# Re-placing the attention and token-mixing steps between the channel-mixing matmuls of a fused pooling-attention and MLP-mixer kernel

## The chip, the cores and the metric

The kernel runs on one core of one Trainium2 chip. Times are device microseconds (us) of one execution. Of several executions of a kernel the median is quoted. Executions of one program mostly agree within a few tenths of a per cent; a few are 1 to 2% longer, at a slightly lower granted clock of TensorE (0.987 to 0.993, where the others have 0.997 to 1.0), and these slow ones are left out of every comparison. The kernel before took 280.01 us (median of 3 runs, 279.32 to 280.36).

Engines: PE is TensorE (matrix products and transposes), DVE is VectorE, ACT is ScalarE, POOL is GpSimd, SP issues transfers. "L258" is line 258 of the kernel.

## The reference, cut to what matters

```python
# q, k, v: [8 batches, 8 heads, 576, 64]
k_p = k.reshape(B, H, 72, 8, D).mean(axis=3)          # keys and values pooled by 8
v_p = v.reshape(B, H, 72, 8, D).mean(axis=3)
attn = softmax(q @ k_p^T / 8)                          # 576 x 72
x = concat_heads(attn @ v_p)                           # [8, 576, 512]
h = relu(x^T @ w_tok1) @ w_tok2                        # token mixing, 576 -> 256 -> 576
u = x + h^T
out = u + relu(u @ w_ch1) @ w_ch2                      # channel mixing, 512 -> 1536 -> 512
```

The channel mixing of one batch is 96 matmuls of 512 columns, about 20.7 us of TensorE. All the rest of a batch takes far less of TensorE, but it takes DVE, ACT and GpSimd as well.

## The kernel before: the parts that the argument touches

The channel mixing of batch n is "unit n". It is cut into 48 steps of two matmuls each, 0.43 us a step. Between the steps the kernel places pieces of the other work for the batches that follow, so that TensorE always has something to do while the other engines prepare. Unit 8 is the rows that are left over from all batches.

```python
ps_one = ... tile_pool(bufs=3, space=PSUM)   # products of 512 columns
ps_two = ... tile_pool(bufs=2, space=PSUM)   # scores and AV, two banks each
ps_tr  = ... tile_pool(bufs=1, space=PSUM)   # transposes: one buffer for all of them
...
def unit_steps(n, st):                       # the stream: 48 steps of two matmuls
    for m in range(NM):                      # NM = 12
        ps = ps_one.tile([P, 512], FP32, name="p1")
        for kk in range(4):
            nc.tensor.matmul(out=ps, lhsT=w_ch1[...], rhs=uT[:, kk, :], ...)        # L445
            if kk == 1:
                yield
        nc.scalar.activation(out=GT[:, m, :], in_=ps, func=AF.Relu)                 # L449
        yield
    ...                                      # then 48 matmuls with w_ch2, L467, and the stores
def unit(n, at):                             # `at` is the plan: step -> pieces
    for i, _ in enumerate(unit_steps(n, ...)):
        for s in at.get(i, "").split():
            ...   # "<x": for batch n, "x": for batch n+1, ">x": for batch n+2; "lk3": load k of batch n+3
```

The pieces that a plan can name, as they are in both kernels:

```python
K0 K1 V0 V1   pool8: three adds on GpSimd for half the heads (L145, L146, then L149 or L151)
Q0..Q3        qD: 32x32 block transposes of the queries on DVE (L246)
kpT           four transposes of the pooled keys on TensorE (L194), a copy to SBUF on ACT (L196)
s0 s1 s2      score4 on 32-row tiles of the array (L258, tile_position=(l*32, 0)): 8 matmuls of 512
              columns in s0 and s1, 16 of 64 in s2; then two exponentials on ACT (L263)
av0..av4      8 matmuls exp x values (L297), then reciprocal and product on DVE (L309, L315)
at0 at1       first token mixing: 5 matmuls (L343), then a relu on ACT (L334) or DVE (L336)
u0..u4        second token mixing: 2 matmuls (L358), then the addition of x on DVE (L359)
t0..t4        four transposes of u on TensorE (L368), a copy on DVE (L369)
M0 M2 M4 M    the other way of transposing u: written to HBM, read back in blocks ("bounce"),
T0..T4        then block transposes on DVE (L390)
lk lq lv      loads of k, q and v, issued from GpSimd's queue
```

Every engine works through its pieces in the order of the plan. A plan therefore fixes who waits for whom.

The softmax here doesn't subtract the row's maximum and nothing guards it: scores larger than these inputs give would overflow.

## Time and profile before

| | before |
|---|---|
| median time | 280.01 us |
| profiled span | 278.3 us |
| TensorE busy, by the page | 97% |
| units 1 to 6, by the trace | 174.61 us |
| of this the floor (instructions times their quiet spacing) | 169.10 us |
| lost in units 1 to 6 | 5.51 us |

The prediction below shows how the floor was counted. Two things of the page help to read it. Here are, of the kernel before, the row of the chain that ended last by engine, and two rows of the costliest groups (count, then busy us and mean ns of one, then idle time before and what ended it):

```profile
PE 83%; DMA 8%; ACT 3%; DVE 2%; POOL 2%; issue 1%; POOLq 0%
...
L449 ACT ACTIVATE GT<-p 128x512 bf16<-128x512 f32 x108 | 64.0, 599 | 75.8 <-PE p L445 75.6
...
L359 DVE TENSOR_TENSOR u<-p,x 128x512 bf16<-128x512 f32 x32 | 22.1, 691 | 13.9 <-PE p L358 13.6
```

TensorE is only 83% of the chain: in the rest something else held the end back, part of it in the head and unit 0, part in small waits in the units. The two rows give the time that ACT (599 ns) and DVE (691 ns) need to empty a PSUM bank of 512 columns.

### The profile page before, as it was taken

The numbers are of one execution on the slowest core, as the hardware profiler recorded it, in microseconds if no ns is written. First come the engines' busy times: TensorE is split into PE (matmuls) and PEld (weight loads), VectorE is DVE, ScalarE is ACT, GpSimd is POOL, SyncE is SP. The second block draws the span as 40 slices with busy tenths as digits, with TensorE's granted clock in tenths as the row PEclk, the third lists the DMA queues.
The fourth block names the chain that finished last, engine by engine and source line by source line (L and its number), as shares of the span: only waits on it lengthen the run. The fifth ranks groups of instructions, "written<-read, shape, count | busy, mean of one in ns | idle before, by whom it ended". The sixth has DMA issues, their size and how long they took to land.

```text
span 278.3 us, 4495 instructions
## 1 busy us (share of the span) xinstructions
PE 268.9 (97%) x1790; PEld 130.9 (47%) x1824; DVE 141.8 (51%) x272; ACT 111.2 (40%) x187; POOL 130.8 (47%) x121
## 2 busy tenths in 40 slices
PE   8989999999999999999999999999999999999994
PEld 3755445444543545454445444544454444444443
DVE  5465967771575757275178545834584161011012
ACT  2543590039305533614741366046604602602600
POOL 8585222999996992898069999600000000000000
PEclk9999999999999999999999999999999999999999
DMA  7999999980299930793549562324132545015024
GB/s 162 185 203 206 205 203 187 225 179 10 24 180 180 231 50 0 138 218 89 115 74 241 144 129 49 77 66 126 38 78 57 136 71 115 0 39 113 2 44 108
DMA packets 36837, 32.68 MB, mean 117 GB/s; under 512 B 14288, under 2 KB 30288, under 8 KB 36816
## 3 DMA queue, kind: packets, MB, share of 16 engines
q0 software_dynamic: 18672, 17.64, 40.2%
q1 hardware_dynamic: 17984, 14.62, 20.9%
q8 instruction: 14, 0.23, 0.3%
q10 hardware_dynamic: 160, 0.13, 0.2%
q14 instruction: 7, 0.06, 0.1%
HBM read 38.21 MB, written 11.80 MB: 180 GB/s over the span
## 4 chain that ended last, share of the span: by engine, by line
PE 83%; DMA 8%; ACT 3%; DVE 2%; POOL 2%; issue 1%; POOLq 0%
PE p L467 32%; PE p L445 30%; PE p L358 6%; PE p L343 5%; DMA kr<-in_k_dram 5%; PE p L258 4%; PE p L297 3%; DMA f<-in_moe_w_tok_dram 3%; ACT ex L263 1%; PE pt L368 1%; PE p L479 1%; ACT GT L449 1%; DVE o L453 1%; POOL vr L86 1%; POOL kr L86 1%
## 5 line engine op out<-in xcount | busy, mean ns | idle before, releaser
L467 PE MATMUL p<-w_ch,GT 128*128 128x512 bf16 x404 | 99.2, 379 | 1.0 <-issue 0.3
L449 ACT ACTIVATE GT<-p 128x512 bf16<-128x512 f32 x108 | 64.0, 599 | 75.8 <-PE p L445 75.6
L445 PE MATMUL p<-uT,w_ch 128*128 128x512 bf16 x373 | 92.7, 379 | 1.1 <-issue 0.3
L445 PEld LDWEIGHTS <-w_ch 128*128 128x128 bf16 x432 | 40.3, 98 | 48.1 <-issue 4.9
L467 PEld LDWEIGHTS <-GT 128*128 128x128 bf16 x420 | 38.0, 98 | 41.9 <-issue 3.1
L453 DVE TENSOR_TENSOR o<-p,u 128x512 f32<-128x512 f32 x32 | 21.9, 684 | 31.4 <-PE p L467 31.2
L263 ACT ACTIVATE ex<-p 72x1024 bf16<-72x1024 f32 (+1 forms) x42 | 31.6, 807 | 10.8 <-PE p L258 10.8
L146 POOL TENSOR_TENSOR t<-t 72x512 f32<-72x512 f32 x24 | 30.3, 1262 | 1.9
L145 POOL TENSOR_TENSOR t<-kr 72x1024 f32<-72x1024 bf16 x12 | 25.5, 2123 | 8.5 <-DMA kr<-in_k_dram 7.8
L359 DVE TENSOR_TENSOR u<-p,x 128x512 bf16<-128x512 f32 x32 | 22.1, 691 | 13.9 <-PE p L358 13.6
L145 POOL TENSOR_TENSOR t<-vr 72x1024 f32<-72x1024 bf16 x12 | 25.4, 2120 | 0.9
L390 DVE STREAM_TRANSPOSE uT<-v 128x512 bf16<-128x512 bf16 x16 | 10.4, 686 | 23.7 <-DMA v<-mem 23.7
L334 ACT ACTIVATE AT<-p 128x512 bf16<-128x512 f32 x8 | 4.8, 597 | 42.0 <-PE p L343 39.2
L315 DVE TENSOR_TENSOR x<-p,den 128x512 bf16<-128x512 f32 x30 | 20.7, 691 | 1.0
L246 DVE STREAM_TRANSPOSE qD<-qb 128x576 bf16<-128x576 bf16 x28 | 20.5, 794 | 0.0
L297 PEld LDWEIGHTS <-ex 72*128 72x128 bf16 x320 | 15.3, 98 | 10.4 <-DVE x L315 0.8
L358 PE MATMUL p<-AT,w_tok 128*128 128x512 bf16 x63 | 18.8, 379 | 0.0
L297 PE MATMUL p<-vp,ex 72*128 72x65 bf16 x320 | 16.8, 194 | 1.0 <-DVE x L315 0.6
L309 DVE RECIPROCAL den<-p 128x8 f32<-128x8 f32 (+1 forms) x39 | 7.9, 203 | 17.5 <-PE p L297 16.6
L103 POOL DMA_DIRECT2D qb<-in_q_dram x7 | 5.1, 730 | 21.5 <-DVE qD L246 20.3
L343 PE MATMUL p<-x,w_tok 128*128 128x512 bf16 x54 | 14.1, 379 | 0.1
L336 DVE TENSOR_SCALAR AT<-p 128x512 bf16<-128x512 f32 x8 | 5.5, 692 | 13.4 <-PE p L343 12.6
(90 smaller groups left out, 206.4 us busy)
## 6 DMA issues: line engine op xcount, KB each, us to landing
out_dram<-o SPq DMA_DIRECT2D x70, 128.0 KB, 2.5
kr<-in_k_dram POOLq DMA_DIRECT2D x7, 576.0 KB, 11.8
qb<-in_q_dram POOLq DMA_DIRECT2D x7, 576.0 KB, 11.1
vr<-in_v_dram POOLq DMA_DIRECT2D x7, 576.0 KB, 15.2
w_ch<-in_moe_w_ch_dram POOLq DMA_DIRECT2D x6, 512.0 KB, 13.2
mem<-u SPq DMA_DIRECT2D x8, 256.0 KB, 2.1
v<-mem SPq DMA_DIRECT2D x8, 160.0 KB, 3.8
v<-mem SPq DMA_DIRECT2D x8, 128.0 KB, 3.0
```

Source lines behind the costliest of these rows:

```text
L145: eng.tensor_tensor(out=t4[:, 0:n], in0=t[:, hs, 0:4], in1=t[:, hs, 4:8], op=ALU.add)
L146: eng.tensor_tensor(out=t4[:, 0:n, 0:2], in0=t4[:, 0:n, 0:2], in1=t4[:, 0:n, 2:4], op=ALU.add)
L263: nc.scalar.activation(out=exv[:, a, :, gs.start:gs.stop, n0:n0 + n], in_=pss[a][0:SP, :, 0:len(gs) * n].rearrange("j l (g n) -> j l g n", ...
L297: nc.tensor.matmul(out=halves[h // 4][:, (h % 4) * (D + 1):(h % 4 + 1) * (D + 1)], lhsT=st["ex"][:, h * S + n0:h * S + n0 + P], rhs=st["vp ...
L315: nc.vector.tensor_tensor(out=dst.rearrange("p (a h d) -> p a h d", a=2, d=D), in0=view[:, :, :, 0:D], in1=den[rows, :, :, None].broadcast ...
L343: nc.tensor.matmul(out=ps, lhsT=w_tok1[:, c if c < 4 else 4 + par, m * P:(m + 1) * P], rhs=st["x"][:, c, :] if c < 4 else st["xt"], start= ...
L358: nc.tensor.matmul(out=ps, lhsT=w, rhs=a, start=(i == 0), stop=(i == len(mms) - 1))
L359: nc.vector.tensor_tensor(out=dst, in0=ps, in1=x, op=ALU.add)
L445: nc.tensor.matmul(out=ps, lhsT=w_ch1[:, kk, m * P:(m + 1) * P], rhs=uT[:, kk, :], start=(kk == 0), stop=(kk == 3))
L449: nc.scalar.activation(out=GT[:, m, :], in_=ps, func=AF.Relu)
L453: nc.vector.tensor_tensor(out=o_sb, in0=ps, in1=(u_tails if n == B else st["u"])[:, c, :], op=ALU.add)
L467: nc.tensor.matmul(out=pss[c], lhsT=GT[:, m, c * P:(c + 1) * P], rhs=w_ch2[:, m, :], start=(m == 0), stop=(m == NM - 1))
```

## The change

The intent is to place the pieces by a model of when each engine gets to them, so that TensorE meets nothing unfinished. Only the plans of units 1 to 8 are different; `HEAD` and `FIRST` (head and unit 0) are wrapped in other places of the text and have the same words. Both programs have the same 1,824 matmuls, loads and stores. `LATER` serves units 4 to 8; in 7 and 8 no later batch is left to place.

```diff
-    SECOND = {0: "Q0 Q1", 1: "kpT Q2 Q3 >K0 >K1 lk3 lq3 lv3 >V0 >V1", 4: "s0", 8: "s1", 13: "s2", 15: "av0", 17: "av1",
-              19: "av2", 21: "av3", 23: "av4", 25: "at0", 26: "at1", 28: "u0", 29: "u1", 30: "u2 t0", 32: "u3 t1", 34: "t2 >Q0",
-              36: "t3 >Q1", 38: ">Q2 >Q3", 39: ">kpT", 40: ">s0 lk4 lq4 lv4", 44: ">s1"}
-    THIRD = {0: ">K0 >K1 >V0 >V1 s2", 2: "av0", 4: "av1", 6: "av2", 8: "av3", 10: "av4", 12: "at0 >Q0", 13: "at1",
-             15: "u0", 16: "u1", 18: "u2 t0", 19: "u3", 20: "t1 u4", 22: "t2 >Q1", 24: "t3", 26: "t4", 27: ">Q2 >Q3",
-             28: ">kpT lq4 lk4 lv4", 29: ">s0", 33: ">s1", 37: ">s2", 39: ">av0", 41: ">av1", 43: ">av2", 45: ">av3", 47: ">av4"}
-    FOURTH = {0: ">K0 >K1 >V0 >V1 at0", 1: "at1", 3: "u4 M4", 4: "u0", 6: "u1 M0", 7: "u2", 9: "u3 M2 M",
-              15: ">Q0", 17: ">Q1", 18: ">kpT", 22: ">s0", 26: "T0", 27: ">Q2 >Q3 lq4 lk4 lv4", 29: "T1", 31: "T2", 32: ">s1",
-              33: "T3", 35: "T4", 37: ">s2", 39: ">av0", 41: ">av1", 43: ">av2", 45: ">av3", 47: ">av4"}
-    LATER = {0: ">K0 >K1 >V0 >V1 at0", 1: "at1", 3: "u4 M4", 4: "u0", 6: "u1 M0", 7: "u2", 9: "u3 M2 M",
-             15: ">Q0", 17: ">Q1", 18: ">kpT", 22: ">s0 >Q2", 24: ">Q3", 27: ">s1", 28: "T0", 30: "T1", 31: "T2",
-             33: ">s2 T3", 35: "T4", 37: ">av0", 39: ">av1", 41: ">av2", 43: ">av3", 45: ">av4"}
+    SECOND = {0: ">K1 Q0 lq3 kpT Q1 Q2", 1: "lv3", 3: "s0 lk3 >V0", 4: ">K0", 6: "Q3 >V1", 8: "s1", 13: "s2",
+              16: "av1 av0", 19: "av2", 20: "av3", 22: "av4", 24: "at1 at0", 26: "u0", 28: ">Q0", 29: "u1", 30: "t0",
+              31: "u2", 32: "t1", 33: "u3 t2", 35: "t3", 36: ">Q1", 37: ">kpT", 38: "lq4", 39: ">s0 >Q2",
+              40: ">Q3 lv4", 44: ">s1", 45: "lk4"}
+    THIRD = {0: ">V0 >K1", 1: "s2", 2: ">K0 >V1", 3: "av0 av1", 6: "av3", 7: "av2", 9: "av4", 10: "at0",
+             12: "at1 >Q0", 15: "u0", 16: "u1", 17: "u2 t0", 18: "u4", 19: "t1", 21: "u3", 22: "t2", 24: ">Q1",
+             25: "t3", 27: "lq4 >kpT", 28: "lv4", 29: "lk4 >Q3 >s0 >Q2", 32: "t4", 33: ">s1", 38: ">s2", 40: ">av0",
+             41: ">av2", 43: ">av1", 45: ">av3", 47: ">av4"}
+    FOURTH = {0: "M4 u4 >K1", 1: "at0 at1 >K0", 3: "u0 >V0", 5: "u1 M0", 6: ">V1", 7: "u2", 8: "u3 M2", 9: "M",
+              15: ">kpT >Q1", 17: ">Q0", 22: "lq4", 25: ">Q2", 26: ">s0", 27: "T0", 28: ">Q3 lk4 lv4", 29: "T1",
+              32: ">s1 T2", 34: "T3", 37: ">s2", 38: "T4", 39: ">av0", 41: ">av1", 42: ">av2", 45: ">av3", 46: ">av4"}
+    LATER = {0: ">K1 at0", 1: "at1", 2: ">V1", 3: "u1 >V0", 5: "u0 u2 u4 >K0", 7: "M0 M4", 9: "u3", 10: "M2", 11: "M",
+             14: ">Q0", 17: ">Q1", 20: ">kpT", 22: ">s0", 25: ">Q2", 26: ">Q3", 27: "T0 >s1", 28: "T3", 31: "T2 T1",
+             35: ">s2", 37: ">av1 >av0", 38: "T4", 41: ">av2", 45: ">av3", 46: ">av4"}
```

In words: the key transposes and the first score group of unit 1 come one step earlier; AV of unit 1 starts one step later after the third score group; u and t pieces are spread; key transposes and first scores of the next batch get more distance; the last score group and AV of units 4 and 5 are closer together; in units 3 to 6 the u pieces are shifted against the channel mixing; query loads go before value and key loads; pools come in another order in all of units 1 to 5.

## The prediction

> **What bounds the kernel now.** I read four views in this order: the page's busy shares and slices, the busy time by window cut at the borders of the nine units of channel mixing, the chain that ended last, and the waits with the timeline of each engine around the places where the chain left TensorE. First the page, engine shares and two rows of its 40 slices:
>
> ```profile
> PE 268.9 (97%) x1790; PEld 130.9 (47%) x1824; DVE 141.8 (51%) x272; ACT 111.2 (40%) x187; POOL 130.8 (47%) x121
> PE   8989999999999999999999999999999999999994
> PEclk9999999999999999999999999999999999999999
> ```
>
> TensorE (PE) is busy in every slice, the clock is full, and no other engine is over 51%. The ends of matmuls are modelled, though, so 97% does not say how much is left. For that I took the distance from one matmul's start to the next. Pieces of the chain (start us, length us, what):
>
> ```profile
> 59.31 0.29 PE pt L194 x4
> 59.60 1.30 PE p L445 x6
> 60.90 0.61 PE p L258 x8
> 61.51 1.91 ACT ex L263 x2
> ...
> 67.66 0.28 ACT ex L263
> ...
> 85.20 0.41 ACT kD L196
> ...
> 88.11 0.80 PE p L258 x8
> ...
> 122.87 0.68 DVE xt L315
> ...
> 136.58 0.56 PE p L258 x8
> ...
> 157.21 0.51 PE p L358 x2
> 157.72 0.43 PE p L445 x2
> ...
> 216.63 6.04 PE p L445 x28
> ```
>
> 28 matmuls of 512 columns took 6.04 us: 0.2157 us each when nothing is missing. The same reading gives 0.0325 us for an AV matmul (8 in 0.26), 0.056 for a 128-column transpose, 0.13 for the four key transposes (L194), 0.56 for a quiet score group of 512 columns and 0.26 for one of 64 (144.38, x16). The reader should see the exceptions: a score group of 0.80 instead of 0.56, a pair L358 of 0.51 instead of 0.43, and pieces of ACT and DVE, where TensorE stood waiting.
>
> Now the windows of units 1 to 6 (window, length, busy us and count by engine, clock, DMA share, GB/s):
>
> ```profile
> 58.26:90.14 31.88, 31.11 (x225) 14.24 (x228) 17.74 (x34) 15.38 (x25) 28.29 (x24) 1.00 0.61 105
> 90.14:122.09 31.95, 31.47 (x265) 16.05 (x270) 19.81 (x41) 13.72 (x23) 24.72 (x20) 1.00 0.63 120
> 122.09:150.20 28.11, 27.90 (x193) 12.83 (x193) 15.48 (x31) 12.41 (x20) 17.40 (x15) 1.00 0.59 127
> 150.20:179.33 29.13, 28.72 (x196) 13.23 (x197) 17.88 (x35) 12.41 (x20) 26.84 (x21) 1.00 0.56 119
> 179.33:207.24 27.91, 27.59 (x187) 12.84 (x190) 15.73 (x30) 12.41 (x20) 0.00 (x0) 1.00 0.31 76
> 207.24:232.87 25.63, 25.44 (x118) 11.55 (x119) 10.09 (x16) 7.66 (x13) 0.00 (x0) 1.00 0.40 88
> ```
>
> **The floor of each unit** is its instructions times those spacings. Unit 1: 96 channel matmuls 20.72, ten of the first token mixing 2.16, eight of the second 1.73, 16 transposes 0.89, two key transposes 0.26, four score groups of 512 columns 2.24, one of 64 0.26, forty AV 1.30: 29.56 us. In the same way units 2 to 6 come to 30.96, 27.41, 28.29, 27.41 and 25.47. Taken from the window lengths this leaves 2.32, 0.99, 0.70, 0.84, 0.50 and 0.16, together **5.5 us that units 1 to 6 lose**. Units 7 and 8 run at the floor; head and unit 0, 58.26 us, aren't changed.
>
> **What the Trainium skill says.** "TensorE: Matmul & The Clock Gate", section "Back-to-back issue gap", gives N / 2.4 + 2.5 ns for a warm matmul, 215.8 ns at N = 512; the trace agrees (215.7). The same section puts a sustained stream with weight loads at about 131 ns; this stream has a weight load per matmul and doesn't reach it. "Perfetto Trace Analysis", "Identifying the Most-Contended Engine", says that matmul busy share is no measure of the room left; the trace agrees, as a matmul is listed at 379 ns and the next starts after 216. Its "Optimization Strategy" says that a gap that repeats can mean too few PSUM buffers; the 0.51 above is one. "PSUM — Partial Sum Buffer", "Engine vs sequencer instructions", says that the queues of ACT, DVE and GpSimd are strictly first in, first out, and that matmuls start in program order. The trace agrees: a query load sat up to 9.9 us at the head of GpSimd's queue until DVE's transposes of the queries had freed its buffer. So order decides who waits, and the change is one of order alone.
>
> **The change.** The programs of both kernels hold the same instructions: 1,824 matmuls, the same loads and stores, no byte more. It can't lower the floor, only move the 5.5 us. Of them about 0.10 us go at the entry of each of 18 score groups (steps of the actual time against the floor, also where no engine was late): 1.8 us, in both kernels. At most 3.7 us can be won. By unit (a plan's step is two matmuls, 0.43 us; positions are floor time since the unit began, and I chose to compare such distances rather than to add up waits of other engines):
>
> - Unit 1, front. The transposes of the keys move from step 1 to step 0, to 0.43 us, but their PSUM buffer is freed by a DVE copy that ended at 59.25, about 1.0 into the unit. Their wait grows from 0.19 to some 0.62: a loss of 0.43. The first score group still waits for the second query transpose (near 60.8). In return the second score group no longer meets unfinished exponentials (0.25), nor does the third (0.19), and AV starts 1.56 after the third score group instead of 1.13, which saves most of the 0.38 of the wait at 67.66. Net about +0.1.
> - Unit 1, rear. A u/t pair is spread (0.08 + 0.17 + 0.19), and key transpose to score goes from 0.56 to 1.00, where transpose, copy and score need some 0.8 (0.22 lost at 85.20 today). The next group comes 2.71 after it instead of 2.28, so that two exponentials of 1.93 together fit between (0.25 at 88.11). DVE will be dense there; I leave 0.25. Net +0.5.
> - Unit 2: key transpose to score 0.56 to 0.99 (0.22), score to score 2.28 to 2.51 (0.25). Net +0.45.
> - Units 3 and 4: the tail of x came late to the first token mixing, 0.21 and 0.36 (the chain's 122.87 and its like at 151.12). Unit 3 now starts that mixing 0.43 later, and unit 3's own last AV, for unit 4, is issued 0.43 earlier. At the end of unit 4 the last AV is 0.43 later, at 27.59 of 28.29: with one reciprocal (0.21) and two products of 0.69 behind it x is there about 0.9 into unit 5, before it is read at 1.30. Net +0.55.
> - Units 3 to 6, u steps: today a matmul reuses a PSUM bank 1.08 after the bank's last matmul and DVE's add of 691 ns stands between, which misses by 0.08, twice in a unit. In the new order the reuse at 1.08 is of a bank that ACT empties in 597 ns, which fits. Four units at 0.16: +0.6.
>
> Sum: 0.1 + 0.5 + 0.45 + 0.55 + 0.6 = 2.2 us. I take off 0.2 for new small waits: **2.0 us, 278.0 us**.
>
> **Rivals.**
> 1. GpSimd becomes the bound. In units 4 and 5 the new order pools K1, V1, V0, K0, where it was K0, K1, V0, V1, so the keys are complete after four pools instead of two. One pool is 2.12 + 1.26 + 0.72 plus gaps, 4.34 us. For it: unit 4's pools queue behind the query load that waits for DVE (began 141.56, now about 0.7 earlier, as one transpose leaves the way). With two more issues of about 0.8 they start near 143.3 and end near 160.7. Against it: the key transposes stand at 13.81 in a unit that begins at 150.2, near 163.5. Slack is about 3 us; if the load slips behind the bounce by 5 us, 2 us are lost and the time is 280.
> 2. DVE gets stuck. The block transposes of the bounced u come first in line one step earlier (27), and wait for the same transfer, issued after the same last add (DVE stood 23.7 us in four such waits already). Query transposes placed behind them would hold up scores. In units 4 and 5 all four now stand ahead; in unit 3 one stays behind, but the score group that needs it hasn't moved (18.82). Cost if I misjudge: about 0.5 us in each of three units, 279.
> 3. The exponentials come late for AV. In unit 4 AV followed the small score group by 1.99, in the new order by 1.12. At the same 1.12 in unit 2 the trace shows AV at 117.34 without a wait, because ACT had no relu in its queue. Same here; else 0.2 a unit.
> 4. Transfers move the time. Query loads go ahead of value and key loads and start up to 4 us earlier; the keys they feed are needed a unit later, and the DMA share in these windows is 0.31 to 0.63. Hidden either way.
>
> **Range and chances.** All waits won that can be: 276.3. Nothing won, or rival 1 or 2 eating the gain: 280. A wait missed in every unit of three: 281. Runs of one kernel spread by 1 us here (279.32 to 280.36). I set 278.0, with 276.8 to 279.8 for 8 in 10. Faster by over 2% needs 5.6 us, more than all that is lost in the changed units above the score entries, 3.7: chance 0.01. Slower by over 2% needs a systematic stall of about 1 us in each changed unit; I found no chain that gives it: 0.02.
>
> **What would show it.** PE's busy share stays at 97% and counts stay the same. Units 1 to 6 should be about 31.3, 31.5, 27.75, 28.65, 27.75 and 25.5 us long. Key transposes at the head of unit 1 should wait longer than 0.19; ACT's exponentials, the copy of the keys and the tail of x should leave the chain from unit 2 on; pairs of L358 should take 0.43. The prediction is wrong if a key transpose waits for a pool in unit 4 or 5, if a score group waits for a query transpose after unit 1, or if AV waits for exponentials in units 4 and 5.

## The result, and the profile after

| | before | after |
|---|---|---|
| median, fast runs | 280.23 us (6 runs, 279.32 to 280.45) | 277.38 us (5 runs, 276.67 to 277.46) |
| slow runs left out | none | one, 283.1 us |
| ratio of fast runs, after / before | | 0.9896, 95% interval 0.9877 to 0.9915 |
| profiled span | 278.3 us | 275.7 us |
| lost in units 1 to 6 | 5.51 us | 2.80 us |

A ratio here is the mean time of one kernel's fast runs over the mean of the other's fast runs in the same rounds on the same chip; it is therefore not quite the ratio of the medians. The change takes 1.0% off. 277.4 lies in the predicted range of 276.8 to 279.8, 0.6 us below the 278.0.

Of the kernel after, two rows of the page: the busy shares (those of before are in the prediction) and the chain that ended last by engine:

```profile
PE 268.2 (97%) x1824; PEld 130.4 (47%) x1824; DVE 141.4 (51%) x272; ACT 111.3 (40%) x187; POOL 130.9 (47%) x121
...
PE 94%; DMA 2%; DVE 2%; issue 0%; POOL 0%; ACT 0%; POOLq 0%
```

The busy share of TensorE is the same 97% to the digit, and tells nothing of the gain. The chain tells more: ACT has left it, and TensorE has gone from 83% to 94%. But about half of this rise lies in the unchanged head and unit 0, where the chain of after runs through 5.6 us of loads instead of 22.6. From unit 1 on, ACT and DVE hold 12.2 us of the chain before and 1.4 us after. A chain shows what held the end back, not how much was lost; that is read from the units.

The trace of before lists 1,790 of its 1,824 matmuls, that of after all of them. A missing record makes a piece look as if it waited, so I read the waits of both from the starts of neighbouring instructions.

The windows of units 1 to 6 of the kernel after (window, length, busy us and count by engine in the order PE, weight loads, DVE, ACT, POOL, then clock, DMA share, GB/s):

```profile
58.36:89.29 30.93, 30.45 (x230) 14.05 (x229) 17.62 (x34) 15.30 (x25) 26.32 (x22) 1.00 0.62 103
89.29:120.71 31.42, 31.42 (x272) 15.86 (x270) 19.54 (x40) 13.82 (x23) 23.34 (x19) 1.00 0.63 114
120.71:148.46 27.75, 27.75 (x196) 12.86 (x193) 15.82 (x30) 12.56 (x20) 20.39 (x17) 1.00 0.71 148
148.46:177.06 28.60, 28.60 (x196) 13.24 (x195) 17.24 (x34) 12.41 (x20) 25.67 (x20) 1.00 0.52 112
177.06:204.79 27.73, 27.73 (x191) 12.82 (x190) 15.58 (x30) 12.41 (x20) 0.00 (x0) 1.00 0.33 79
204.79:230.26 25.47, 25.47 (x119) 11.53 (x118) 10.64 (x18) 7.66 (x13) 0.00 (x0) 1.00 0.40 88
```

Each line answers to one of the six in the prediction. The lengths sum to 171.90 us against 174.61, a gain of 2.71. Unit 1 begins 0.10 later than in before (58.36 against 58.26), and from the end of unit 6 to the end both take 45.4. So 2.71 less 0.10 is the 2.6 us between the spans: **the gain lies in the six changed units and nowhere else**.

| unit | length before | predicted | after | lost before | lost after |
|---|---|---|---|---|---|
| 1 | 31.88 | 31.3 | 30.93 | 2.32 | 1.37 |
| 2 | 31.95 | 31.5 | 31.42 | 0.99 | 0.46 |
| 3 | 28.11 | 27.75 | 27.75 | 0.70 | 0.33 |
| 4 | 29.13 | 28.65 | 28.60 | 0.84 | 0.32 |
| 5 | 27.91 | 27.75 | 27.73 | 0.50 | 0.32 |
| 6 | 25.63 | 25.5 | 25.47 | 0.16 | 0.00 |

The front of unit 1 in the chain of the kernel after (start us, length us, what):

```profile
59.41 0.29 PE pt L194 x4
59.71 1.30 PE p L445 x6
61.00 0.56 PE p L258 x8
61.56 2.27 PE p L445 x10
...
68.34 0.52 PE p L297 x16
```

The score group at 61.00 takes its quiet 0.56 (0.61 in before) and is followed by matmuls, where before had ACT's exponentials on the chain at 61.51. At 67.66 before had an exponential ahead of AV; here AV runs at its quiet pace. Left in this part is only the wait ahead of the key transposes at 59.41.

### The profile page after: what moved, and what is told of

It is laid out like the page before. It is cut to its first block, busy times and chain, and to the rows that moved or that the text cites. A ratio compares the mean times of both kernels' runs of the same rounds, so it can differ in the third digit from the quotient of the medians.

```text
span 275.7 us, 4525 instructions
## 1 busy us (share of the span) xinstructions
PE 268.2 (97%) x1824; PEld 130.4 (47%) x1824; DVE 141.4 (51%) x272; ACT 111.3 (40%) x187; POOL 130.9 (47%) x121
## 4 chain that ended last, share of the span: by engine, by line
PE 94%; DMA 2%; DVE 2%; issue 0%; POOL 0%; ACT 0%; POOLq 0%
PE p L445 34%; PE p L467 33%; PE p L358 6%; PE p L343 5%; PE p L297 4%; PE p L258 4%; DMA kr<-in_k_dram 2%; PE pt L368 1%; PE p L479 1%; PE p L225 1%; PE pt L515 1%; PE p L277 1%; PE p L326 1%; PE p L408 1%; PE p L203 1%
## 5 line engine op out<-in xcount | busy, mean ns | idle before, releaser
L467 PE MATMUL p<-w_ch,GT 128*128 128x512 bf16 x420 | 101.3, 379 | 0.0
L145 POOL TENSOR_TENSOR t<-kr 72x1024 f32<-72x1024 bf16 x12 | 25.5, 2121 | 6.7 <-DMA kr<-in_k_dram 5.9
L145 POOL TENSOR_TENSOR t<-vr 72x1024 f32<-72x1024 bf16 x12 | 25.5, 2121 | 0.8
L297 PEld LDWEIGHTS <-ex 72*128 72x128 bf16 x320 | 14.7, 98 | 9.1 <-DVE x L315 1.1
L358 PE MATMUL p<-AT,w_tok 128*128 128x512 bf16 x64 | 18.5, 379 | 0.0
L334 ACT ACTIVATE AT<-p 128x512 bf16<-128x512 f32 x8 | 4.8, 597 | 34.1 <-PE p L343 31.3
L297 PE MATMUL p<-vp,ex 72*128 72x65 bf16 x320 | 16.1, 194 | 0.5 <-DVE x L315 0.3
L258 PE MATMUL p<-qD,kD 32*72 32x512 bf16 (+1 forms) x224 | 11.4, 294 | 0.0
```

The source lines that it names most:

```text
L145: eng.tensor_tensor(out=t4[:, 0:n], in0=t[:, hs, 0:4], in1=t[:, hs, 4:8], op=ALU.add)
L258: nc.tensor.matmul(out=pss[l // 2][0:SP, l % 2, i * n:(i + 1) * n], lhsT=st["kD"][quad, g, db, :], rhs=st["qD"][quad, g, db, n0:n0 + n], s ...
L297: nc.tensor.matmul(out=halves[h // 4][:, (h % 4) * (D + 1):(h % 4 + 1) * (D + 1)], lhsT=st["ex"][:, h * S + n0:h * S + n0 + P], rhs=st["vp ...
L358: nc.tensor.matmul(out=ps, lhsT=w, rhs=a, start=(i == 0), stop=(i == len(mms) - 1))
L467: nc.tensor.matmul(out=pss[c], lhsT=GT[:, m, c * P:(c + 1) * P], rhs=w_ch2[:, m, :], start=(m == 0), stop=(m == NM - 1))
```

## The experiments

Eleven kernels were run, on three chips in three groups; all gave correct results. Kernels of one group ran on the same chip with runs of the kernel before among them. All the edits are of plans, but for one. This table is the key to all of them. "Lost" is a unit's length in the profiled run less its floor, as above; "ahead" is what head and unit 0 lost, counted in the same way up to the start of unit 1.

| kernel | group | lost in units 1, 2, 3, 4, 5, 6 | sum | ahead | median of fast runs | ratio to before, 95% |
|---|---|---|---|---|---|---|
| before | all | 2.32 0.99 0.70 0.84 0.50 0.16 | 5.51 | 5.82 | 280.1 to 280.3 | 1 |
| after | own | 1.37 0.46 0.33 0.32 0.32 0.00 | 2.80 | 5.93 | 277.38 | 0.9896, 0.9877 to 0.9915 |
| e1_unit1 | 1 | 1.36 1.19 0.70 0.84 0.48 0.16 | 4.73 | 6.28 | 279.53 | 0.9963, 0.9929 to 0.9996 |
| e2_units2to6 | 1 | 2.33 0.47 0.33 0.32 0.32 0 | 3.77 | 6.40 | 278.35 | 0.992, 0.9895 to 0.9944 |
| e3_pool_queue | 1 | 2.33 1.00 0.70 0.84 0.48 0.16 | 5.51 | 6.18 | 280.32 | 0.9986, 0.9962 to 1.001 |
| e4_rest | 1 | 1.36 0.46 0.33 0.32 0.32 0 | 2.79 | 7.85 | 277.57 | 0.9889, 0.9863 to 0.9915 |
| e5_u_steps | 2 | 2.34 1.00 0.56 0.68 0.33 0 | 4.91 | 5.97 | 279.72 | 0.9984, 0.9966 to 1.0002 |
| e6_exp_spacing | 2 | 1.36 0.46 0.33 1.00 1.00 0 | 4.15 | 6.30 | 279.17 | 0.997, 0.9952 to 0.9988 |
| e7_key_step | 2 | 1.12 0.46 0.33 0.32 0.32 0 | 2.55 | 5.83 | 277.13 | 0.9899, 0.9884 to 0.9915 |
| e8_tuned | 2 | 0.77 0.46 0.33 0.32 0.32 0 | 2.20 | 6.12 | 277.06 | 0.9893, 0.9878 to 0.9908 |
| e9_entries | 3 | units 4 and 5 +0.68 and +0.69 over after | | | 279.15 | 0.9956, 0.9939 to 0.9972 |
| e10_tuned2 | 3 | 0.89 0.46 0.33 0.32 0.32 0 | 2.32 | 5.95 | 276.83 | 0.9876, 0.9861 to 0.9891 |
| e11_after_again | 3 | 1.36 0.46 0.33 0.32 0.32 0 | 2.79 | 5.70 | 277.39 | 0.9898, 0.9882 to 0.9914 |

The table shows at what precision each reading can be trusted. What a unit loses repeats to 0.02 us between runs and chips. What is lost ahead of unit 1 varies from 5.7 to 6.4 with no change of plan behind it (7.85 in one run, explained below). One slow run each of e1 and e4 (283.06 and 283.37 us) is left out of the medians. So the execution time of one run varies by about as much as any single effect here, and I take effects from the units and use times only to check their sum.

### e1_unit1 and e2_units2to6: two halves

The first kernel is before with the new plan of unit 1, the second is before with the new plans of all the other units. They ask whether each half has its own gain, as the prediction's sum takes for granted.

```diff
 e1_unit1: before
-    SECOND = {0: "Q0 Q1", 1: "kpT Q2 Q3 >K0 >K1 ...
+    SECOND = {0: ">K1 Q0 lq3 kpT Q1 Q2", 1: "lv3", ...          # that of after
 e2_units2to6: before
-    THIRD, FOURTH, LATER of before
+    THIRD, FOURTH, LATER of after
```

> The kernel before with the new plan of unit 1 alone. Theory (the time is the sum of TensorE's own waits, unit by unit): unit 1 shortens from about 32.1 us to 30.9 as in the changed kernel, units 2 to 6 keep their lengths of before within 0.15 us each, and the time falls by 1.2 us (0.4%). Rival A (the order of loads and pools on GpSimd's queue made the gain, over all units): the time falls by about a quarter of 2.8 us or less, and unit 1 stays over 31.5. Rival B (the gain is a drift of the clock or of the two traces): no change of unit 1.

> The complement: new plans from unit 2 on, the plan of unit 1 as before. Theory: unit 1 stays near 32.1 us, units 2 to 6 come to 31.4, 27.75, 28.6, 27.75 and 25.5, the time falls by 1.5 us (0.55%), and the falls of this run and of the one before add up to the whole change (2.7 to 2.9 us) within 0.4. Rival A or an interaction between the plans: the two do not add up.

Unit 1 lost 1.36 with its new plan and 2.33 with the old one; units 3 to 6 lost the same in e2 as in after. But the halves do not quite add up: e1 saves 0.78 and e2 1.74, together 2.52, where the whole change saves 2.71. This is inside the 0.4 that e2's expectation allowed, but ten times what units repeat to. The missing 0.19 is in unit 2 of e1, which loses 1.19 instead of 0.99, outside the 0.15 that e1's expectation allowed. Here is its border in the timeline of e1 (start us, length us, engine, line, operation, what ended the idle time before):

```profile
88.44 1.93 ACT L263 ACTIVATE ex<-p 72x1024 bf16<-72x1024 f32 x2 [0.89 <-PE p L258]
...
90.17 0.58 PE L258 MATMUL p<-qD,kD 32*72 32x64 bf16 x16
```

The exponentials of unit 1's last score group run until 90.37. The small score group that opens unit 2 needs the PSUM buffers that they read, and it stands from 90.17, taking 0.58 by the timeline; by the same view it took 0.38 in before and 0.33 in after. A score group of unit 1 that no longer waits comes closer to the next one, four steps on, so part of the wait moves over the border. The new plan of unit 2 has `s2` at step 1 instead of 0; both together let it pass. A wait removed in one plan had to be paid for in the next, by one step.

### e3_pool_queue and e4_rest: is it GpSimd's order?

Loads and pools were the most visible part of the rewritten plans. e3 is before with GpSimd's pieces (pools and loads) in the order of after, and all pieces of the other engines in before's order; e4 is the reverse. That only GpSimd's order differs was checked instruction by instruction.

```diff
 e3_pool_queue: before                               e4_rest: after
-    LATER = {0: ">K0 >K1 >V0 >V1 at0", 1: "at1", 3: "u4 M4", ...
+    LATER = {0: ">K1 at0", 1: "at1", 2: ">V1", 3: ">V0 u4 M4", 4: "u0", 5: ">K0", ...
     (loads and pools of the other plans in the same way; in e4_rest the other way round)
```

> The kernel before with only the loads and pools moved, so that GpSimd's queue has exactly the order of the changed kernel; TensorE, DVE and ACT keep the order of before. Theory: no gain, time within 0.4 us of before, the sum lost in units 1 to 6 stays near 5.5 us. Rival A (loads and pools made the gain): the time falls by 1.5 to 2.8 us. Rival C (the new order of the queue is a cost that the other moves hide): the time rises by over 0.5 us.

> The changed kernel with loads and pools put back to the steps of before: the moves on TensorE, DVE, ACT and the bounce alone. Theory: the whole gain stays, 2.7 to 2.9 us (1.0%), and units 1 to 6 lose 2.8 us together as in the changed kernel, within 0.3. Rival A: the gain goes, 0 to 1 us.

e3 gained nothing: 5.51 us lost as in before, ratio 0.9986 with 1 inside the interval. e4 kept all of the gain: 2.79 us lost, ratio 0.9889. The order of pools and loads is worth nothing either way.

One run of e4 was 2 us longer than the rest, and it was the profiled one. Its timeline of TensorE shows why:

```profile
31.25 1.06 PE L225 MATMUL p<-kr,ident 72*72 72x256 bf16 x8 [1.69 <-DMA kr<-in_k_dram]
```

TensorE waited 1.69 us for the keys of batch 1 in unit 0, which no plan here had changed. In the other traces with that plan of unit 0 that I looked at it waited 0.27 or 0.40 us there (before, e2) or not at all. Had I compared spans of single profiles, e4 would have shown the gain as gone (277.6 against after's 275.7).

### e5_u_steps: the PSUM bank of the second token mixing

This is before with the new places of u and M pieces in units 3 to 6 alone.

```diff
-    FOURTH = {0: ">K0 >K1 >V0 >V1 at0", 1: "at1", 3: "u4 M4", 4: "u0", 6: "u1 M0", 7: "u2", 9: "u3 M2 M", ...
+    FOURTH = {0: ">K0 >K1 >V0 >V1 at0", 1: "at1", 3: "u0", 5: "u1 M0", 7: "u2", 8: "u3 M2", 9: "M", ...
-    LATER  = {0: ">K0 >K1 >V0 >V1 at0", 1: "at1", 3: "u4 M4", 4: "u0", 6: "u1 M0", 7: "u2", 9: "u3 M2 M", ...
+    LATER  = {0: ">K0 >K1 >V0 >V1 at0", 1: "at1", 3: "u1", 5: "u0 u2 u4", 7: "M0 M4", 9: "u3", 10: "M2", 11: "M", ...
```

> The kernel before with only the second token mixing (u) and the stores of the bounce moved to their new steps in the plans from unit 3 on. Theory (a PSUM bank reused 1.08 us after its last matmul misses by 0.08 when DVE's 691 ns add empties it, and fits when ACT's 597 ns relu does): the two waits of 0.08 in each of units 3 to 6 go, so these units lose 0.16 less each, 0.6 us in all, about 0.2% of the time. Rival (the 0.08 is a cost of switching between the two products, as it stands before an L445): the waits stay and the time with them. In the trace the pieces L358 x2 of 0.51 us become 0.43.

The window of unit 4 (as above; before has 29.13):

```profile
150.25:179.21 28.96, 28.77 (x200) 13.23 (x197) 17.77 (x35) 12.43 (x20) 27.28 (x21) 1.00 0.57 123
```

Units 3 to 6 lose 0.14, 0.16, 0.17 and 0.16 less, 0.63 together, for the 0.6 of the prediction, and the two waits of 0.08 in each unit are gone. The ratio of times, 0.9984, has the right sign, but its interval ends at 1.0002: by the times alone this experiment is inconclusive, by the units it isn't. That the bank's buffer is the cause fits the durations (a bank is wanted again 1.08 us after its last matmul, and goes through with ACT's 599 ns in between but not with DVE's 691). No run changed the number of buffers by itself.

### e6_exp_spacing: the distance between score groups

The prediction put gains in units 1 and 2 down to score groups far enough apart for two exponentials. This run takes that distance away where the new plan has it: in units 4 and 5 the second score group comes two steps earlier, three after the first, not five.

```diff
-    LATER = {... 22: ">s0", 25: ">Q2", 26: ">Q3", 27: "T0 >s1", 28: "T3", ...
+    LATER = {... 22: ">s0", 23: ">Q2", 24: ">Q3", 25: ">s1", 27: "T0", 28: "T3", ...
```

> The changed kernel with the second score group of units 4 and 5 two steps earlier (25 instead of 27), and its query transposes before it. The distance to the first group falls from 2.71 to 1.85 us of floor time. Theory (the group waits for two exponentials of together 1.93 us, which need a distance of about 2.53): each of the two units gains a wait of 0.68 us, units 4 and 5 grow from 28.6 and 27.7 to 29.3 and 28.4, the time by 1.35 us. Rival (distance does not matter, the old 0.25 had another cause): no growth.

```profile
164.42 1.92 ACT ex L263 x2
```

This line of e6's chain is new: between the first score group of unit 4, which ends at 164.42, and the next there is now 1.92 us of ACT in the chain of what ended last. Units 4 and 5 are each 0.68 us longer than in after, and the time rises by 1.8 us against after's (of which 1.36 is in the units; the rest is ahead of unit 1, as the table shows). A wait of TensorE of this kind costs what it is, one to one.

### e7_key_step: the one loss that was predicted

The prediction said that the key transposes, moved to step 0 of unit 1, would wait 0.62 instead of 0.19 us for the PSUM buffer of transposes. This run is after with this one piece moved back.

```diff
-    SECOND = {0: ">K1 Q0 lq3 kpT Q1 Q2", 1: "lv3", ...
+    SECOND = {0: ">K1 Q0 lq3 Q1 Q2", 1: "kpT lv3", ...
```

> The changed kernel with the key transposes of unit 1 back at step 1. Theory (they wait for a PSUM buffer that DVE frees about 1.0 us into the unit): their wait falls from 0.62 to 0.19 us, unit 1 from 30.92 to 30.5 if nothing later takes it back; the first score group, 1.43 behind, may then wait for the second query transpose, which ends at about the same time, and take back up to 0.2. Rival (the wait is for the keys from GpSimd): no change.

From the chain of e7; the lines of after at the same place (59.41 and 61.00) stand above:

```profile
59.33 0.29 PE pt L194 x4
59.62 0.86 PE p L445 x4
60.48 0.75 PE p L258 x8
```

The wait fell from 0.62 to 0.19, by 0.43 as told. Of this 0.19 came back: the first score group, at 60.48 in this run, then took 0.75 instead of 0.56, because the second query transpose was not done. The net is 0.24 us, with unit 1 losing 1.12. DVE's timeline has that transpose end at 60.77 in this run, and the half of the group that reads it starts at 60.82. In after it ends at 60.85 and that half starts at 61.18, so there it can't hold the group up.

### e9_entries: what a score group costs beyond its matmuls

Of the 2.80 us that remain in after I had put 1.8 down to the entry into 18 score groups, 0.10 each, in both kernels. To test whether it is a cost per entry, this run cuts the small score group of units 4 and 5 into four parts of four matmuls, with two channel matmuls between parts. The matmuls are the same.

```diff
+        name["p0"] ... name["p3"] = part(0) ... part(3)    # 4 of the 16 matmuls of s2 each; exponentials with p3
-    LATER = {... 31: "T2 T1", 35: ">s2", 37: ">av1 >av0", 38: "T4", ...
+    LATER = {... 31: "T2 T1", 33: ">p0", 34: ">p1", 35: ">p2", 36: ">p3", 38: ">av1 >av0 T4", ...
```

> The changed kernel with the small score group of units 4 and 5 (16 matmuls of 64 columns) cut in four parts of four matmuls, one step apart, with the exponentials after the last and AV one step later. Same work. Theory (some 0.10 us, and 0.15 of the group's own time, are paid at every entry into a score group from full-array matmuls, so that the prediction was right to call 0.10 for each of 18 groups out of reach of an order that keeps their number): three more entries a unit at about 0.25, units 4 and 5 grow by 0.7 to 0.75 us each, the time by 1.45. Rival (the 0.10 is a wait for data, or hidden when parts are small): no growth, or under 0.3 in all.

From the chain of e9 (line 277 is the part, and line 489 what is line 467 elsewhere):

```profile
169.94 0.16 PE p L277 x4
170.09 0.54 PE p L489 x2
```

Units 4 and 5 took 29.28 and 28.42 us, 0.68 and 0.69 more than in after, which is 0.23 us for each of three more entries. The lines show its two halves. Four small matmuls take 0.16, a quarter of the whole group 0.065; four parts thus take 0.38 more than the group, 0.13 for each added entry. And the pair of full-size matmuls behind a part takes 0.54 instead of 0.43, 0.11 more. So the entry costs more than my 0.10: the 0.10 was only what shows behind the group, and the other 0.13 sat in the small group's own 0.26, which I had counted as floor (that the groups of 512 columns have the same in their 0.56 is likely, not shown). It is the same in both kernels; order cannot take it away, and fewer groups were not tried.

The Trainium skill has this in "TensorEngine Tiling (Array Packing)", section "Key Properties": changing the tiling mode, as against the tile, drains TensorE. The score matmuls use 32-row tiles and all the others the whole array, so each group is such a change and back. The trace agrees with a cost at each change; that it is a drain, the trace doesn't show.

### e8_tuned, e10_tuned2 and e11_after_again: is there more?

Knowing the waits, I tried to take more of them away by order alone, in unit 0 as well. e8 is after with these moves; e10 goes on from there; e11 is after once more, beside e10 on the same chip.

```diff
 e8_tuned: after
     FIRST:  kpool1 4 -> 7, s1 17 -> 18, s2 22 -> 23, av0 24 -> 25, t3 45 -> 46, t4 removed
     SECOND: >Q0 >Q1 >Q2 >Q3 all at 10, <t4 at 14, u3 33 -> 32
 e10_tuned2: after
     FIRST:  kpool1 4 -> 7, s1 17 -> 18, s2 22 -> 23, av0 24 -> 26, t1 42 -> 41, t2 44 -> 43, u4 and t4 removed
     SECOND: >K0 4 -> 3, >V0 3 -> 4, <u4 at 5, >Q0 >Q1 >Q2 >Q3 all at 10, <t4 at 14, >kpT 37 -> 25, u3 33 -> 32
```

> A version meant to beat both: the changed kernel with the waits that its trace still shows taken away. The tail transpose of unit 0 moves into unit 1 (so the key transposes find a free PSUM buffer: 0.62), unit 0's last transpose and its second score group are spaced as in the other units (0.25 each), unit 1's query transposes run early when DVE is idle and its third u step goes one step forward (0.19), and the pool that TensorE does in unit 0 stands three steps later, behind the landing of its keys (0.1 to 1.8, it varies from run to run). Theory: 1.3 to 1.7 us faster than the changed kernel, 0.985 of the time before. Rival: the dense stretch of DVE in unit 0 makes new waits of the same size.

> The second try at a version that beats both. The first one left three waits: AV after its exponentials in unit 0 (0.38), unit 1's first product after unit 0's last transpose (0.25), key transposes after the last transpose of unit 1 (0.19). Here AV of unit 0 starts one step later in a pair, the transposes of unit 0 stand two steps apart and the tail's u goes to unit 1 with its transpose, and unit 1's key transposes stand at step 25, ahead of the other transposes, with the keys pooled second on GpSimd. Theory: the three waits go, units 1 to 6 lose about 2.0 us and unit 0 0.7, the time is 0.8 us below the first try and about 1.1 below the changed kernel. Rival: the waits move again.

> The changed kernel once more, on the same chip as the two others, for their comparison. Expected: the ratio of its first measurement, 0.990, and the same waits to 0.02 us in units 1 to 6 (2.8 us in all); unit 0 and the head may differ, as the landing of the first keys does.

e8 took 0.60 us out of unit 1, but the time fell by only 0.3 against after's in another group, which is inside the spread; 1.3 to 1.7 had been expected. The trace shows new waits: in unit 0 AV now stands 0.38 us for an exponential that sits in ACT's queue behind relus, the first product of unit 1 waits 0.25 us for the transpose that now comes last in unit 0, and key transposes late in unit 1 wait 0.19 us. e10 repaired these in part. Its remaining waits are of the same kinds: by the starts of matmuls 0.26 us at the first score group of unit 1, and 0.36 us at the end of unit 0, which the timeline of TensorE shows in part as idle time:

```profile
55.14 0.38 PE L368 MATMUL pt<-ident,u 128*128 128x128 bf16 x4 [0.19 <-DVE uT L369]
```

The transposes of u have one PSUM buffer, and two sets in close succession wait for DVE's copy of the first. On one chip e10 took 276.83 us (276.48 to 277.04, 4 runs) and e11, the change as it is, 277.39 (277.04 to 277.83, 4 runs): 0.56 us, half of the 1.1 that I had expected. e10 beats the change by 0.2% there, and before by 1.2%. Its median is the lowest, but e7 and e8 (277.13 and 277.06 us) ran on another chip, so it is not shown that it beats them. e11 has the waits of the first run of after to 0.01 us.

## Why the prediction was right, point by point

**What bounds it.** The reading that TensorE is the bound, with 5.5 us lost in units 1 to 6 and nothing else to win, held. The gain is in those units (2.71 us), and the same instructions at the same spacing make the rest.

**The sum.** Predicted for the units: 2.2, less 0.2 for new waits. Measured: 2.71.

| step of the prediction | predicted | measured |
|---|---|---|
| unit 1, front | +0.1 | +0.36 |
| unit 1, rear | +0.5 | +0.61 |
| unit 2 | +0.45 | +0.53 |
| tail of x in units 3 and 4 | +0.55 | +0.60 |
| u steps of units 3 to 6 | +0.6 | +0.63 (e5) |
| new small waits | -0.2 | about -0.05, counted in unit 1, front |
| sum | 2.0 | 2.7 |

Unit 1 is split behind the first AV. The trace of before lacks records there, so I read the split from e5, which has before's plan of unit 1 and all its records: up to the first AV it loses 1.33 us and after 0.97, behind it 1.03 and 0.42. (The lengths in the table above give 0.95 for the two together.) Units 3 to 6 gained 1.23 together (0.37, 0.52, 0.18 and 0.16); less e5's 0.63 that leaves 0.60 for the tail of x, which no run isolated.

**The term that was mis-sized is the front of unit 1.** The prediction lists its parts: a loss of 0.43 at the key transposes, gains of 0.25 and 0.19 at the second and third score groups, and most of 0.38 at AV. The parts sum to as much as 0.39, and the trace gives nearly that: the four waits of before were 0.19, 0.25, 0.19 and 0.38, 1.01 in all, and after has the 0.62 at the key transposes and a new one of some 0.05 at the third score group. I had written down +0.1, because I let the first score group keep a wait for the second query transpose. It has none: in after the transpose ends at 60.85 and the half of the group that reads it begins at 61.18, because the longer wait at the key transposes comes ahead of it. I had read that wait partly from a place in before's trace where a matmul record is missing. The 0.2 for new waits was the second error, in the same direction. Together they are over half of the 0.7 us by which the units gained more than predicted; the rest is 0.03 to 0.11 in each of the other rows.

In the rear, the prediction's own parts come to 0.66 (0.91 less the 0.25 that it leaves), not 0.5, and 0.10 of its 0.22 at 85.20 is the entry of the score group, which stays. What it leaves stayed too, but as one of the u and t waits that were to go: in after, `t3` stands 0.19 us at 82.42 for DVE's copy of `t2`, which ends at 82.37. That the row came near its +0.5 is luck in that part: the reserve covered a wait that it was not meant for.

**The loss at the key transposes** was predicted at 0.62 instead of 0.19 and is exactly that; e7 shows that undoing it is worth 0.24, not 0.43, since the next wait is just behind.

**Rival 1, GpSimd becomes the bound**: no. e3 and e4 show that its order is worth nothing either way. In after the query load was issued at 138.57 (before 141.56; I had expected 0.7 earlier, it was 3.0), the fourth pool of unit 4's keys ended at 158.24, and the key transposes came at 162.43. The slack is 4.2 us, where I had said 3.

**Rival 2, DVE gets stuck on the bounce**: no. Units 3 to 5 lose 0.32 or 0.33 each, which is three score entries at 0.10 and next to nothing.

**Rival 3, exponentials late for AV in units 4 and 5**: no. AV's 16 matmuls at 171.60 took 0.52, their quiet time, although it follows the small score group by 1.23 us there.

**Rival 4, transfers**: the DMA shares in the windows moved by up to 0.12 (0.59 to 0.71 in unit 3) and the units didn't lengthen. Hidden, as said. The one place where a transfer was seen not to be hidden, the keys of batch 1 in unit 0, is in a plan that the change leaves alone.

**The signs.** From unit 2 on the chain of after holds nothing but TensorE, and all pairs of L358 take 0.43. Beyond the entries of score groups no wait of TensorE in units 2 to 5 is over 0.03 us. So none of the three things that the prediction named as proving it wrong happened.

**What it did not foresee.** The units are not independent: e1's unit 2 lost 0.20 more because unit 1 had become faster. The prediction summed units as if they were, and was right only because the change has the matching step in unit 2.

**What stays open.** What makes the 0.6 us of spread ahead of unit 1 was not tested. Neither was whether one more PSUM buffer for transposes would take the waits at L194 and L368 away.

## What to carry to other kernels

When one engine is the bound and only order changes, count its instructions at their quiet spacing, take that from the length of each stage in the trace, and you have the most that any reordering can win; here 5.5 us of 280, or 3.7 without the entries into score groups, which stay in any order. The change took 2.7. Then follow each wait to the next one behind it before writing down its worth, since removing 0.43 gave 0.24 in one place and moved 0.20 into the next stage in another. Judge effects of a few tenths of a microsecond from stages of the trace, which repeat to 0.02 us, rather than from times that vary by 0.5.

## What the Trainium skill lacked or had wrong

- "TensorE: Matmul & The Clock Gate", section "Back-to-back issue gap", puts a sustained stream of weight load and matmul at about 131 ns for N = 512. In this kernel 28 such matmuls in a row took 6.04 us, 215.7 ns each, at the full granted clock and with a weight load for each; the formula that the section gives for a matmul by itself, 215.8 ns, is the one that holds.
- "TensorEngine Tiling (Array Packing)", section "Key Properties", says that a change of tiling mode drains TensorE but gives no price. Each added group of 32-row tiles in a stream of full-array matmuls cost 0.23 us (e9: 0.68 and 0.69 us for three), of which 0.11 shows in the pair of matmuls behind it.
- No page that I found gives the turn-around of a PSUM bank, from the last matmul into it to the first of its next use. Here a reuse 1.08 us after the start of the last matmul went through where ACT emptied the bank (599 ns for 128x512), and was 0.08 us late where DVE did with an addition (691 ns).
